# A fused linear-attention and gated-MLP block: GpSimd subtracts the means itself, 29 small operations on other engines, new orders and banks

## The chip, the core and the metric

The kernel runs on one core of a Trainium2 chip. The core has a matrix engine (TensorE, PE in the profile), three elementwise engines (VectorE or DVE, ScalarE or ACT, GpSimd or POOL) and a queue that issues transfers (SyncE, SP). Each engine works through its own list of instructions in order; engines wait for each other on semaphores. The metric is the device time of one execution in microseconds (us).

## The reference, cut to what matters

```
x = A_x                                  # 2048 x 448, bf16
n = layernorm(x)                         # no gain, no bias
q, k, v = split(n @ wqkv)                # 16 heads of 28
phi(t) = where(t > 0, t + 1, exp(t)) + 1e-6
kv  = sum over tokens of phi(k)^T v      # per head
z   = sum over tokens of phi(k)
o   = (phi(q) @ kv) / (phi(q) . z + 1e-6)
h   = x + o @ wo
h2  = h + (gelu(layernorm(h) @ w_gate) * (layernorm(h) @ w_up)) @ w_down
```

`w_gate` and `w_up` are 448 x 1792, `w_down` is 1792 x 448.

## The kernel before, in words

**Tiles.** The 2048 tokens are 16 tiles of 128. 448 columns are three blocks of 128 and one of 64; most products therefore use half of TensorE's rows (64) and run two at a time, one on each half, with a first pass ("a", 8 products) and a second pass ("b", 6 products) that adds to the same two PSUM banks with the halves exchanged. PSUM has eight banks of 128 x 512 f32.

**Tasks and names.** The kernel first builds a graph of 955 tasks. A task has an engine, the buffers that it reads and writes, and a name; on the three elementwise engines a task is one instruction. The names used below, with tile number t:

- `ast`/`aag` t: mean and variance of x (VectorE, L412, L413). `anm`: the negated means of a group (GpSimd, L417), of the tile pairs from tile 2 on. `aln`/`ars`: 1/sqrt(var) by logarithm and exponential (ScalarE, L422, L424).
- `norm` t: (x - mean) * rstd. Tiles 0 and 1 on VectorE (L454, subtract the mean), the others on GpSimd (L457, add the negated mean). `dup` t: for odd tiles, the last 64 columns are copied a second time (L461, L464), as the transposing transfer and the v products need it.
- `tr` t, `ev` t: tiles 0 to 3 are transposed on TensorE (L472 to L474) and copied out of PSUM (VectorE L479 for 0 and 1, ScalarE L481 for 2 and 3). The others go two at a time by a transposing transfer, `xT` (L483).
- `ks` 0, 1 (L506) and `ka`/`kb` t (L519): the k products. `ek` t: exp (ScalarE, L492); `cl` t: clamp to at most 1 (GpSimd, L493); `ph` t: phi(k) (VectorE, L494).
- `g0a`, `g0b`, `g2a`, `g2b` t: the sums over tokens of phi(k) with the normalised x, in four banks (L543). `evg` c copies them out (L568, L570); `zbm`, `evz` spread z over the partitions (L572, L573); `kvp` multiplies by the v weights (L582); `kz1` masks heads (L590); `mm` k multiplies by wo (L601) and `evm` k copies out (L605, L607). So kv and wo become one 448 x 448 matrix.
- `qa`/`qb` t (L620), `eq` t, `cq` t, `pq` t: the same phi for q (L628 to L630).
- `mul` t: phi(q) times z (GpSimd, L660); `den` t, `rd` t: sum per head and reciprocal (VectorE, L662, L663); `om` t: phi(q) divided by the sum (GpSimd, L666).
- `tro`, `evo`, `wo` 0 and 1: transposition on TensorE and product for tiles 0 and 1 (L679 to L694); `oT` (L698), `woa`/`wob` for the other pairs (L705).
- `hr` t: h = x + product (VectorE, L714). `bst`, `bag`: its mean and variance. 1/sqrt for tiles 0 and 1 on ScalarE (`bln`, `brs`), for the pairs after them on GpSimd (`bve`, L429, and `bpw`, a power, L431), with the negated means in `bnm` (L417).
- `normh` t: tiles 0 and 1 on VectorE (L727), then `trh` on TensorE (L734, L736) and `evh` (L739); the others on GpSimd (L746), then `wrap` t, a copy of the last 64 columns (VectorE, L748), and a transposing transfer, `hT` (L749).
- `gua`/`gub` v (L818, L821): gate and up products; `ge` v (ScalarE, L844): gelu; `hm` v (VectorE, L846): times up. The tokens go in chunks of 2, 2, 4, 4 and 4 tiles; v counts 0 to 6 in the first chunk, 7 to 13 in the second, then 14 a chunk.
- `da`/`db` t (L768), `down` (L782), `out` t (VectorE, L788), `dout` t (L790): the down product of a pair of tiles, the last addition and the store. Tiles 14 and 15 go singly, tile 15 in two halves of 224 columns.

**What sets the order.** A list of task numbers for each engine (`ORDERS`, one string each for TensorE, ScalarE, VectorE, GpSimd and SyncE) and a list of banks (`BANKS`, one for each of 196 PSUM tiles), both written into the file. `place` (L155) gives the tasks their order and adds a wait wherever a tile takes a bank that another held: the new product waits for that tile's last reader. `emit` (L204) waits on semaphores by these dependencies and nothing else. Durations and keys in the calls are for the planner that made the lists and change nothing at run time.

**Around the start.** TensorE first does nine products of ones (`warm`, L407), then the four transpositions in the order tr2, tr0, tr1, tr3, then ks1, ks0, ka2, kb2, qa0, qb0, qa2, qb2, ka4, g0a0, kb4. VectorE's list begins with the memset of a part of xn (`xones`, L382, L383), and has that of kvT (`kvzero`, L385, 128 x 1248) behind ph13.

**Around the end of attention.** TensorE: ... kvp qa8 mm0 mm3 mm1 tro1 mm2 qb8 wo1 tro0 qa10 wo0 qb10 qa14 qa12 qb14 qb12 trh1 trh0 woa2 gua3. VectorE: ... den1 rd1 kz1 pq7 den0 pq4 rd0 evm1 den3 pq5 rd3 hr1 bst1 den2 bag1 rd2 pq8 hr0 bst0 pq9 bag0 pq10 normh1 normh0 pq11 evh1. GpSimd: ... cq6 mul1 cq7 mul0 cq4 om1 mul3 cq5 om0 mul2 cq8 om3 om2 cq9 cq10 cq11 mul6 mul7 cq13 cq14 cq12 cq15 om6 mul5 om7 mul4 bve2 bnm2 bpw2 normh2 normh3.

Of the kernel before, what the change touches and what calls it, by code (L numbers as in the profile page):

```python
# [235 lines left out]
def bass_sequential_preLN__linear_attn_block__glu_gated_geglu__prompt_kernel(  # L236
# [27 lines left out]
    with es:
# [657 lines left out]
```

## Time and profile before

| | us |
|---|---|
| median of 3 runs | 194.56 (194.43 to 195.72) |
| the profiled execution | 192.99 |
| its span on the core, from the first instruction to the last | 191.3 |
| TensorE busy | 185.3 |
| VectorE busy | 120.0 |
| GpSimd busy | 78.8 |
| ScalarE busy | 66.5 |

Times in the profile count from the start of the span. L12 is line 12 of the kernel file. A row of the timeline has the start, the duration, the engine, the line, the operation, what it writes and reads, and in brackets the idle time of the engine before it and what ended it; neighbouring instructions of one kind stand in one row (x3). A row of the groups has the busy time of all, the mean of one in ns, and the idle time of the engine before them. In the table by stretch each engine has its busy time and, in brackets, its number of instructions. Ends of products are modelled: two products that follow each other overlap in the rows, so the distance from one start to the next is what a product takes.

### The profile page before, as it was taken

What the parts mean: (1) busy time and instruction counts of PE and PEld (TensorE: products, weight loads), DVE (VectorE), ACT (ScalarE), POOL (GpSimd) and SP (SyncE); (2) the same over time, 40 slices, a digit from 0 to 9 for tenths busy, and PEclk for the clock granted to TensorE, in tenths of its full rate; (3) what the DMA queues carried; (4) which work ended last, traced back from release to release, by engine and by line L of the source; (5) the groups of instructions that cost most, each with busy time, mean ns of one, the idle gap of its engine ahead of it and who ended that gap; (6) DMA issues with size and microseconds to landing.
All of it is one profiled execution on the core that took longest, in us unless ns stands there. A gap on an engine that the chain in (4) does not pass through costs nothing.

```text
span 191.3 us, 4853 instructions
## 1 busy us (share of the span) xinstructions
PE 185.3 (97%) x1939; PEld 108.9 (57%) x1939; DVE 120.0 (63%) x303; ACT 66.5 (35%) x188; POOL 78.8 (41%) x133
## 2 busy tenths in 40 slices
PE   7899999999899999999999999999999999999994
PEld 2334545444499897865555556555555555555643
DVE  4979737598998998387956634374745144345332
ACT  3675624465645241200234330041542321232200
POOL 2899864399899927870129400004600000000000
PEclk9999999999999999999999999999999999999999
DMA  5999589903785122523000382000650000002033
GB/s 139 251 231 176 108 146 319 299 10 87 194 220 122 32 51 48 55 57 55 0 3 0 75 132 28 0 3 0 30 107 26 5 0 0 3 0 72 3 132 108
DMA packets 32694, 15.93 MB, mean 83 GB/s; under 512 B 21536, under 2 KB 32416, under 8 KB 32672
## 3 DMA queue, kind: packets, MB, share of 16 engines
q1 hardware_dynamic: 32672, 15.63, 36.9%
q8 instruction: 15, 0.25, 0.5%
q14 instruction: 7, 0.06, 0.1%
HBM read 8.37 MB, written 1.84 MB: 53 GB/s over the span
## 4 chain that ended last, share of the span: by engine, by line
PE 91%; DVE 4%; POOL 1%; DMA 1%; issue 1%; ACT 0%; POOLq 0%; DVEq 0%
PE ps L818 39%; PE ps L768 19%; PE ps L543 6%; PE ps L821 5%; PE ps L519 5%; PE ps L705 5%; PE ps L620 4%; PE ps L782 3%; DVE st L412 1%; DMA x_sb<-in_A_x_dram 1%; PE ps L506 1%; PE ps L601 1%; POOL xn L457 1%; DVE pq L630 1%; DVE hn L727 1%
## 5 line engine op out<-in xcount | busy, mean ns | idle before, releaser
L821 PE MATMUL ps<-hnT,wgu_sb 64*128 64x512 bf16 (+1 forms) x490 | 87.1, 333 | 0.0
L818 PE MATMUL ps<-hnT,wgu_sb 64*128 64x512 bf16 (+1 forms) x490 | 87.1, 333 | 0.0
L844 ACT ACTIVATE gl<-ps 128x256 bf16<-128x256 f32 x112 | 35.9, 384 | 88.7 <-PE ps L821 56.9
L846 DVE TENSOR_TENSOR hh<-ps,gl 128x256 bf16<-128x256 f32 x112 | 42.1, 415 | 36.2 <-ACT gl L844 35.7
L818 PEld LDWEIGHTS ps<-hnT,wgu_sb 64*128 64x128 bf16 x490 | 46.0, 94 | 30.7 <-issue 0.4
L821 PEld LDWEIGHTS ps<-hnT,wgu_sb 64*128 64x128 bf16 x490 | 45.9, 94 | 0.1
L768 PE MATMUL ps<-wd_sb,hh 64*128 64x448 bf16 x392 | 39.4, 349 | 0.0
L768 PEld LDWEIGHTS ps<-wd_sb,hh 64*128 64x128 bf16 x392 | 22.0, 94 | 15.0 <-issue 0.2
L412 DVE BATCH_NORM_STATS2 st<-x_sb 128x6 f32<-128x448 bf16 x32 | 19.0, 615 | 2.1 <-DMA x_sb<-in_A_x_dram 1.9
L666 POOL TENSOR_TENSOR o<-pq,rd 128x448 bf16<-128x448 bf16 x16 | 15.0, 944 | 12.3 <-DVE rd L663 11.8
L417 POOL TENSOR_SCALAR nm<-mv 128x2 f32<-128x2 f32 (+1 forms) x15 | 3.5, 232 | 32.9 <-DVE mv L413 32.6
L660 POOL TENSOR_TENSOR prod<-pq,zb 128x448 f32<-128x448 bf16 x16 | 16.4, 1034 | 0.0
L788 DVE TENSOR_TENSOR x_sb<-ps,x_sb 128x448 bf16<-128x448 f32 (+1 forms) x17 | 9.9, 590 | 10.1 <-PE ps L768 5.1
L543 PE MATMUL ps<-pk,xn 64*128 64x448 bf16 (+1 forms) x128 | 15.2, 351 | 0.4 <-DVE pk L494 0.4
L494 DVE SCALAR_TENSOR_TENSOR pk<-ps,tm 128x448 bf16<-128x448 f32 x16 | 9.6, 617 | 6.3 <-POOL tm L493 2.5
L714 DVE TENSOR_TENSOR x_sb<-ps,x_sb 128x448 bf16<-128x448 f32 x16 | 9.6, 608 | 6.1 <-PE ps L705 5.6
L620 PE MATMUL ps<-wq_sb,xnT 64*128 64x448 bf16 x112 | 12.7, 350 | 0.1
L519 PE MATMUL ps<-wk_sb,xnT 64*128 64x448 bf16 x98 | 11.8, 350 | 0.1
L705 PE MATMUL ps<-m_sb,oT 64*128 64x448 bf16 x98 | 11.1, 349 | 0.0
L492 ACT ACTIVATE e<-ps 128x448 bf16<-128x448 f32 x16 | 8.0, 540 | 8.3 <-PE ps L519 7.6
L493 POOL TENSOR_SCALAR tm<-e 128x448 bf16<-128x448 bf16 x16 | 8.8, 561 | 4.5 <-ACT e L492 4.4
L457 POOL TENSOR_SCALAR xn<-x_sb,nm,rs 128x448 bf16<-128x448 bf16 x14 | 10.0, 720 | 1.4 <-ACT rs L424 0.9
(80 smaller groups left out, 148.8 us busy)
## 6 DMA issues: line engine op xcount, KB each, us to landing
out_dram<-x_sb SPq DMA_DIRECT2D x15, 112.0 KB, 1.8
wd_sb<-in_B_w_down_dram SPq DMA_DIRECT2D x3, 448.0 KB, 5.1
wgu_sb<-in_B_w_gate_dram SPq DMA_DIRECT2D x3, 384.0 KB, 7.8
wgu_sb<-in_B_w_up_dram SPq DMA_DIRECT2D x3, 384.0 KB, 4.1
x_sb<-in_A_x_dram SPq DMA_DIRECT2D x2, 448.0 KB, 4.6
x_sb<-in_A_x_dram SPq DMA_DIRECT2D x4, 112.0 KB, 2.1
x_sb<-in_A_x_dram SPq DMA_DIRECT2D x2, 224.0 KB, 3.5
wo_sb<-in_A_wo_dram SPq DMA_DIRECT2D x1, 392.0 KB, 7.5
```

The costliest lines, as they stand in the source:

```text
L412: op("dve", lambda e: e.bn_stats(st[:, t, :], src_ap()), [b_src], [b_st[t]], nm + "st%d" % t, 0.615, key)
L519: ins = e.matmul(ps[:, p_k[n].bank, 0:D], xnT[rows, t0 + n, k, :], wk_sb[rows, k, :], start=(k == 0 and not second), stop=(second and k == ...
L543: ins = e.matmul(ps[0:b - a, p_gx[cc].bank, 0:D], xnv(t, a, b)[rows], pk[rows, i, :], start=(t == 0 and not second), stop=(t == T - 1), sk ...
L620: ins = e.matmul(ps[:, p_q[n].bank, 0:D], xnT[rows, ts[n], k, :], wq_sb[rows, k, :], start=(k == 0 and not second), stop=(second and k == ...
L660: op(me, lambda e, ip=ip, p3=p3: e.tensor_tensor(prod[:, ip, :, 0:28], p3(), zb[:].rearrange("p (a e) -> p a e", e=28), ALU.mult), [b_pq[t ...
L666: return e.tensor_tensor(o2[:, so, n, :].rearrange("p (a e) -> p a e", e=28), p3(), rd[:, i, :].unsqueeze(2).to_broadcast([128, 16, 28]), ...
L705: ins = e.matmul(ps[:, p_h[n].bank, 0:D], oT2[rows, so, kk, :], m_sb[rows, kk, :], start=(k == 0 and not second), stop=(second and k == 2) ...
L768: ins = e.matmul(ps[:, p_d[n].bank, 0:D], hh[rows, j, u * 128:(u + 1) * 128], wd_sb[rows, j, :], start=(j == 0 and not second), stop=(j == ...
L818: e.matmul(ps[:, pa.bank, jj * N:(jj + 1) * N], wgu_sb[A_, wa + k if k < 3 else 3, jc], hnT[A_, k, c0:c0 + N], start=(k == 0 and jj == 0 a ...
L821: ins = e.matmul(ps[:, pb.bank, jj * N:(jj + 1) * N], wgu_sb[B_, wb + k if k < 3 else 3, jc], hnT[B_, k, c0:c0 + N], start=(k == 0 and jj ...
L844: G.add("act", lambda e, gi=gi, cs=cs, p_g=p_g: e.activation(gl[:, gi, cs], ps[:, p_g.bank, cs], AF.Gelu_apprx_tanh), r=[p_g], w=[b_gl[gi] ...
L846: op("dve", lambda e, dst=dst, gi=gi, cs=cs, p_u=p_u, rs_=rs_: e.tensor_tensor(dst, rs_(ps[:, p_u.bank, cs]), rs_(gl[:, gi, cs]), ALU.mult ...
```

## The change

Four things change, and nothing else in what is computed.

1. GpSimd's normalisations subtract the mean and multiply, with the mean itself as operand. The negated means (`anm`, `bnm`, 15 instructions on GpSimd) and their buffers go; 940 tasks are left.
2. 29 tasks get another engine, by name (`ENGINE`). From VectorE to GpSimd: norm0, norm1, dup1, normh1. From GpSimd to VectorE: norm2, norm15, cl3, cl8, cl13, cl14, cq4, cq5, cq6, normh2, normh4, normh7. From VectorE to ScalarE: ev0, evg0, evm1, wrap2 to wrap7. From ScalarE to VectorE: ev2, ev3, evz. From ScalarE to GpSimd: dup15.
3. All five orders are new. The start of VectorE's list is now: the memset for prod, kvzero, ast2 ast0 aag2 aag0 ast1 aag1 ast3 aag3 norm2 ast4 ast5 xones aag5 aag4 ev1 ev2 ev3. GpSimd begins with norm0 norm1 norm3 norm5 norm4 cl0 cl1 norm7 dup1 cl2 norm6; its `powwarm` (a first use of the power, L387) moves from before norm3 to before bve2. TensorE: warm tr0 tr2 tr1 ks0 tr3 ks1 ka2 kb2 qa0 g0a0 qb0 qa2 g0b0 qb2 ka4 g0a1 kb4; later ka10 g0b7 g2b7 kb10 g2a8 (before: ka10 g0b7 g2b7 g0a8 g2a8 kb10); then qb6 g0b13 g0a14 zbm g0b14 g0a15 g0b15 qa4 kvp qb4 qa8 mm1 mm2 mm0 tro1 mm3 qb8 tro0 wo1 qa10 wo0 qb10 qa14 qa12 qb14 qb12 trh1 trh0 woa2 gua3. VectorE there: ... evg2 evz cq6 pq7 pq6 den1 kz1 rd1 den0 cq4 rd0 den3 cq5 rd3 pq5 pq4 den2 rd2 hr1 pq9 bst1 hr0 bag1 bst0 pq8 bag0 den6 pq11 normh0 pq10 evh1, and later bag2 bag3 hm3_1 hm3_0 hm0_0 hm0_1 normh2 hm2_1 hm2_0. GpSimd there: cq7 mul1 mul0 mul3 om1 om0 mul2 om3 cq9 om2 cq8 mul6 cq11 cq10 normh1 mul7 cq12 cq14 cq15 om6 cq13 om7 powwarm bve2 bpw2 normh3 mul4 mul5 mul8. SyncE fetches tile 1 of x before tile 3, and issues the transfers of the later weights in another order, some of them later.
4. The banks are new.

The diff, cut to its core (orders and banks left out):

```diff
+ENGINE = (
+    "norm0:pool ev0:act norm1:pool dup1:pool norm2:dve ev2:dve ev3:dve cl3:dve norm15:dve dup15:pool cl8:dve cl13:dve"
+    " cl14:dve evg0:act evz:dve evm1:act cq4:dve cq5:dve cq6:dve normh1:pool normh2:dve wrap2:act wrap3:act normh4:dve"
+    " wrap4:act wrap5:act wrap6:act normh7:dve wrap7:act"
+)
...
+    ENGINE_OF = dict(p.split(":") for p in cfg.get("engine", ENGINE).split())
+
+    def at(name, default):
+        return ENGINE_OF.get(name, default)
+
+    def copy_on(e, eng, o, x):
+        return e.activation(o, x, AF.Identity) if eng == "act" else e.tensor_copy(o, x)
...
-        def ln_negm(ts, mv, nm, b_mv, b_nm, name, key):
-            a, b = ts[0], ts[-1] + 1
-            op("pool", lambda e: e.tensor_scalar(nm[:, a:b], mv[:, a:b, 0], -1.0, None, ALU.mult),
-               b_mv[a:b], b_nm[a:b], name + "%d" % a, 0.225, key)
...
-                if t < N_DVE_NORM:
-                    op("dve", lambda e, t=t: e.tensor_scalar(xnv(t, 0, D), x_sb[:, t, :], mv1[:, t, 0:1], rs1[:, t:t + 1], ALU.subtract, ALU.mult),
-                       [b_x[t], b_mv1[t], b_rs1[t]], [b_xn[sx]], "norm%d" % t, 0.38, kln + 0.05)
-                else:
-                    op("pool", lambda e, t=t: e.tensor_scalar(xnv(t, 0, D), x_sb[:, t, :], nm1[:, t:t + 1], rs1[:, t:t + 1], ALU.add, ALU.mult),
-                       [b_x[t], b_nm1[t], b_rs1[t]], [b_xn[sx]], "norm%d" % t, 0.715, kln + 0.05)
+                ne = at("norm%d" % t, "dve" if t < N_DVE_NORM else "pool")
+                op(ne, lambda e, t=t: e.tensor_scalar(xnv(t, 0, D), x_sb[:, t, :], mv1[:, t, 0:1], rs1[:, t:t + 1], ALU.subtract, ALU.mult),
+                   [b_x[t], b_mv1[t], b_rs1[t]], [b_xn[sx]], "norm%d" % t, 0.40 if ne == "dve" else 0.715, kln + 0.05)
...
-            op("pool", lambda e: e.tensor_scalar(tm1[:, ie, :], e1[:, ie, :], 1.0 + EPS, 0.0, ALU.min, ALU.max), [b_e1[ie]], [b_tm1[ie]], "cl%d" % t, 0.56, kk + 0.3)
+            op(at("cl%d" % t, "pool"), lambda e: e.tensor_scalar(tm1[:, ie, :], e1[:, ie, :], 1.0 + EPS, 0.0, ALU.min, ALU.max), [b_e1[ie]], [b_tm1[ie]], "cl%d" % t, 0.56 if at("cl%d" % t, "pool") == "pool" else 0.45, kk + 0.3)
...
-                ln_negm(list(ts), mv2, nm2, b_mv2, b_nm2, "bnm", k2 + 0.32)
...
+                ne = at("normh%d" % t, "dve" if first else "pool")
+                op(ne, lambda e, t=t, sh=sh: e.tensor_scalar(hn[:, sh, 0:D], h_sb[:, t, :], mv2[:, t, 0:1], rs2[:, t:t + 1], ALU.subtract, ALU.mult),
+                   [b_h[t], b_mv2[t], b_rs2[t]], [b_hn[sh], b_hnd[sh]], "normh%d" % t, 0.59 if ne == "dve" else 0.715, k3)
...
-                    op("dve", lambda e, sh=sh: e.tensor_copy(hn[:, sh, D:512], hn[:, sh, 384:D]), [b_hn[sh]], [b_hnd[sh]], "wrap%d" % t, 0.25, k3 + 0.01)
+                    we = at("wrap%d" % t, "dve")
+                    op(we, lambda e, sh=sh, we=we: copy_on(e, we, hn[:, sh, D:512], hn[:, sh, 384:D]), [b_hn[sh]], [b_hnd[sh]], "wrap%d" % t, {"dve": 0.35, "act": 0.255, "pool": 0.26}[we], k3 + 0.01)
```

The other copies out of PSUM (`ev`, `evg`, `evz`, `evm`, `evo`, `evh`), the clamps `cq`, `dup`, `mul` and `om` look their engine up in the same way.

More of the change, by code (lines that the diff above doesn't have):

```diff
@@ L477, in ln_group @@
                     src = lambda p_t=p_t: psb[:, p_t.bank, 0:512].rearrange("p (k t) -> p k t", k=4)
-                    if t in EV_DVE:
-                        op("dve", lambda e, t=t, src=src: e.tensor_copy(xnT[:, t, :, :], src()), [p_t], [b_xnT[t]], "ev%d" % t, 0.41, kln + 0.12)
-                    else:
-                        op("act", lambda e, t=t, src=src: e.activation(xnT[:, t, :, :], src(), AF.Identity), [p_t], [b_xnT[t]], "ev%d" % t, 0.6, kln + 0.12)
+                    ee = at("ev%d" % t, "dve" if t in EV_DVE else "act")
+                    op(ee, lambda e, t=t, ee=ee, src=src: copy_on(e, ee, xnT[:, t, :, :], src()), [p_t], [b_xnT[t]], "ev%d" % t, 0.41 if ee == "dve" else 0.6, kln + 0.12)
                 elif t % 2:
@@ L566, in bass_sequential_preLN__linear_attn_block__glu_gated_geglu__prompt_kernel @@
             r_ = 128 if c < 3 else 65
-            if c in EVG_DVE:
-                op("dve", lambda e, c=c, r_=r_: e.tensor_copy(gx[0:r_, c, :], ps[0:r_, p_gx[c].bank, 0:D]), [p_gx[c]], [b_gx[c]], "evg%d" % c, 0.62, 27.0 + 0.1 * EVG.index(c))
-            else:
-                op("act", lambda e, c=c, r_=r_: e.activation(gx[0:r_, c, :], ps[0:r_, p_gx[c].bank, 0:D], AF.Identity), [p_gx[c]], [b_gx[c]], "evg%d" % c, 0.546, 27.0 + 0.1 * EVG.index(c))
+            ge = at("evg%d" % c, "dve" if c in EVG_DVE else "act")
+            op(ge, lambda e, c=c, r_=r_, ge=ge: copy_on(e, ge, gx[0:r_, c, :], ps[0:r_, p_gx[c].bank, 0:D]), [p_gx[c]], [b_gx[c]], "evg%d" % c, 0.62 if ge == "dve" else 0.546, 27.0 + 0.1 * EVG.index(c))
         p_zb = G.psum("zb")
         G.add("pe", lambda e: e.matmul(ps[:, p_zb.bank, 0:D], ones_bf[64:65, :], gx[64:65, 3, :], start=True, stop=True), r=[b_ones, b_gx[3]], w=[p_zb], name="zbm", dur=_pe(D, 1, 64), key=27.3, mode=64)
-        op("act", lambda e: e.activation(zb[:], ps[:, p_zb.bank, 0:D], AF.Identity), [p_zb], [b_zb], "evz", 0.546, 27.4)
+        ze = at("evz", "act")
+        op(ze, lambda e: copy_on(e, ze, zb[:], ps[:, p_zb.bank, 0:D]), [p_zb], [b_zb], "evz", 0.62 if ze == "dve" else 0.546, 27.4)
         p_kv = G.psum("kv")
@@ L658, in a2_pair @@
                 p3 = lambda t=t: pq[:, t, :].rearrange("p (a e) -> p a e", e=28)
-                me, se = ("dve" if t in MUL_DVE else "pool"), ("dve" if t in SCL_DVE else "pool")
+                me, se = at("mul%d" % t, "pool"), at("om%d" % t, "pool")
                 op(me, lambda e, ip=ip, p3=p3: e.tensor_tensor(prod[:, ip, :, 0:28], p3(), zb[:].rearrange("p (a e) -> p a e", e=28), ALU.mult), [b_pq[t], b_zb], [b_prod[ip]], "mul%d" % t,
-                   0.60 if me == "dve" else 1.035, k0)
+                   1.30 if me == "dve" else 1.035, k0)
                 op("dve", lambda e, i=i, ip=ip: e.tensor_reduce(den[:, i, :], prod[:, ip, :, :], mybir.AxisListType.X, ALU.add), [b_prod[ip], b_prc], [b_den[i]], "den%d" % t, 0.62, k0 + 0.1)
@@ L738, in a2_pair @@
                     G.add("pe", ftrh, r=[b_hn[sh], b_ident], w=[p_th], name="trh%d" % t, dur=0.40, key=k3 + 0.1)
-                    cp = (lambda e, o, x: e.activation(o, x, AF.Identity)) if t % 2 == 0 else (lambda e, o, x: e.tensor_copy(o, x))
-                    tk = op("act" if t % 2 == 0 else "dve",
-                            lambda e, t=t, p_th=p_th, cp=cp: cp(e, hnT[:, :, (t % HR) * 128:(t % HR + 1) * 128], psb[:, p_th.bank, 0:512].rearrange("p (k t) -> p k t", k=4)),
-                            [p_th], [b_hnT[t % HR]], "evh%d" % t, 0.59 if t % 2 == 0 else 0.41, k3 + 0.2)
-                    if t % 2 == 0:
+                    he = at("evh%d" % t, "act" if t % 2 == 0 else "dve")
+                    tk = op(he, lambda e, t=t, p_th=p_th, he=he: copy_on(e, he, hnT[:, :, (t % HR) * 128:(t % HR + 1) * 128], psb[:, p_th.bank, 0:512].rearrange("p (k t) -> p k t", k=4)),
+                            [p_th], [b_hnT[t % HR]], "evh%d" % t, 0.59 if he == "act" else 0.41, k3 + 0.2)
+                    if he == "act":
                         exp_tasks.append(tk)
                 else:
-                    op("pool", lambda e, t=t, sh=sh: e.tensor_scalar(hn[:, sh, 0:D], h_sb[:, t, :], nm2[:, t:t + 1], rs2[:, t:t + 1], ALU.add, ALU.mult),
-                       [b_h[t], b_nm2[t], b_rs2[t]], [b_hn[sh], b_hnd[sh]], "normh%d" % t, 0.715, k3)
-                    op("dve", lambda e, sh=sh: e.tensor_copy(hn[:, sh, D:512], hn[:, sh, 384:D]), [b_hn[sh]], [b_hnd[sh]], "wrap%d" % t, 0.25, k3 + 0.01)
+                    we = at("wrap%d" % t, "dve")
+                    op(we, lambda e, sh=sh, we=we: copy_on(e, we, hn[:, sh, D:512], hn[:, sh, 384:D]), [b_hn[sh]], [b_hnd[sh]], "wrap%d" % t, {"dve": 0.35, "act": 0.255, "pool": 0.26}[we], k3 + 0.01)
                     G.add("sp", lambda e, t=t, sh=sh: e.dma_start_transpose(hnT[:, :, (t % HR) * 128:(t % HR + 1) * 128], hn[:, sh, :]), r=[b_hn[sh], b_hnd[sh]],
```

39 lines of the change are left out of this document (12 added, 27 removed), and 77 rows, old and new, of tables (BANKS, ORDERS).

## The prediction, made before the result was known

> **What bounds the kernel now.** I read the page first, then the busy time of each engine by stretch, then TensorE's timeline, then the chain of waits.
>
> ```profile
> span 191.3 us, 4853 instructions
> PE 185.3 (97%) x1939; PEld 108.9 (57%) x1939; DVE 120.0 (63%) x303; ACT 66.5 (35%) x188; POOL 78.8 (41%) x133
> ```
>
> ```profile
> core 0: us, PE busy (x) PEld busy (x) DVE busy (x) ACT busy (x) POOL busy (x), PEclk, DMA share, GB/s
> 0.00:5.60 5.60, 4.02 (x9) 1.20 (x9) 3.00 (x11) 2.28 (x5) 1.80 (x12) 1.00 0.59 161
> 5.60:9.50 3.90, 3.57 (x27) 1.63 (x27) 3.89 (x14) 2.73 (x10) 3.15 (x7) 1.00 0.91 247
> 9.50:20.00 10.50, 10.30 (x102) 4.71 (x103) 9.29 (x24) 7.07 (x22) 10.27 (x20) 1.00 0.99 198
> 20.00:32.00 12.00, 11.61 (x124) 6.07 (x120) 6.50 (x14) 4.94 (x14) 7.72 (x16) 1.00 0.77 172
> 40.00:52.50 12.50, 11.54 (x97) 5.21 (x92) 11.91 (x26) 7.75 (x18) 11.72 (x16) 1.00 0.42 105
> 52.50:185.00 132.50, 132.50 (x1480) 83.47 (x1479) 78.19 (x209) 37.35 (x114) 39.82 (x59) 1.00 0.23 44
> 185.00:191.30 6.30, 3.79 (x27) 2.42 (x25) 1.91 (x4) 0.00 (x0) 0.00 (x0) 1.00 0.36 121
> ```
>
> TensorE is the bound. From 52.5 to 185 us it has no idle time at all and its clock is granted in full, so engines and orders can't shorten that part; they can only break it. The last stretch is the final products, the last addition and its store: the change leaves the last three products and the last store in their places. What can move lies before 52.5 us, where attention ends and the gate/up products (L818, L821) start, and where VectorE (11.91 of 12.50 us) and GpSimd (11.72) are full as well. So I ask one thing: when does the first gate/up product (52.52 us) start after the change?
>
> ```profile
> 5.62 0.34 PE L472 MATMUL ps<-ident,xn 128*128 128x128 bf16 x3 [0.53 <-POOL xn L457]
> 6.07 0.34 PE L472 MATMUL ps<-ident,xn 128*128 128x128 bf16 x3
> 7.88 2.00 PE L506 MATMUL ps<-wk_sb,xnT 128*128 128x448 bf16 x8
> 9.53 1.92 PE L519 MATMUL ps<-wk_sb,xnT 64*128 64x448 bf16 x14
> 11.29 3.29 PE L620 MATMUL ps<-wq_sb,xnT 64*128 64x448 bf16 x28
> 14.41 0.92 PE L519 MATMUL ps<-wk_sb,xnT 64*128 64x448 bf16 x8
> 18.73 0.93 PE L519 MATMUL ps<-wk_sb,xnT 64*128 64x448 bf16 x8
> 19.49 0.55 PE L543 MATMUL ps<-pk,xn 64*128 64x448 bf16 x4
> 25.97 0.55 PE L543 MATMUL ps<-pk,xn 64*128 64x448 bf16 x4 [0.39 <-DVE pk L494]
> 50.09 0.34 PE L734 MATMUL ps<-ident,hn 128*128 128x128 bf16 x3 [0.44 <-DVE hn L727]
> 51.11 0.34 PE L734 MATMUL ps<-ident,hn 128*128 128x128 bf16 x3 [0.51 <-DVE hn L727]
> 52.52 0.27 PE L818 MATMUL ps<-hnT,wgu_sb 64*128 64x256 bf16 x1
> ```
>
> Starts tell more than durations, which overlap. Eight 64-row products take 19.49 - 18.73 = 0.76 us when nothing holds them, 0.095 us each. The 28 q products from 11.29 to 14.41 take 3.12 us where 28 x 0.095 = 2.66 would do. And the rows with brackets are waits for VectorE's phi (L494) and for the normalised h (L727).
>
> **The change, part by part.** Prices, by form:
>
> ```profile
> L417 POOL TENSOR_SCALAR nm<-mv 128x2 f32<-128x2 f32 x13 | 2.9, 225 | 30.1 <-DVE mv L413 29.8
> L457 POOL TENSOR_SCALAR xn<-x_sb,nm,rs 128x448 bf16<-128x448 bf16 x14 | 10.0, 720 | 1.4 <-ACT rs L424 0.9 <-PE ps L543 0.3 <-POOL nm L417 0.2
> L454 DVE TENSOR_SCALAR xn<-x_sb,mv,rs 128x448 bf16<-128x448 bf16 x2 | 0.7, 374 | 0.0
> L727 DVE TENSOR_SCALAR hn<-x_sb,mv,rs 128x448 bf16<-128x448 bf16 x2 | 2.0, 1052 | 0.0
> L493 POOL TENSOR_SCALAR tm<-e 128x448 bf16<-128x448 bf16 x16 | 8.8, 561 | 4.5 <-ACT e L492 4.4
> L479 DVE COPY xnT<-ps 128x512 bf16<-128x512 bf16 x2 | 0.7, 403 | 0.0
> L568 DVE CAST gx<-ps 128x448 bf16<-128x448 f32 x2 | 1.2, 625 | 1.1 <-PE ps L543 1.1
> L748 DVE COPY hn<-hn 128x64 bf16<-128x64 bf16 x14 | 5.5, 397 | 4.6 <-POOL hn L746 4.4
> ```
>
> *Negated means.* Fifteen instructions of about 0.225 us go, 3.4 us of GpSimd. GpSimd's subtract-and-multiply is shown nowhere; the nearest row is its add-and-multiply, 0.72 us, the clamp with two constants at 0.56 us is the other bound, and I take 0.72. Since this time lies beside a full TensorE, it is worth something only where GpSimd ends last: the row of L457 shows 0.2 us of waiting for nm in all. Term: 0, at most -0.2.
>
> *The same VectorE instruction has two prices.* L454 and L727 have the same operation and shape, yet take 0.374 and 1.052 us. The timeline says why:
>
> ```profile
> 48.87 2.05 POOL L660 TENSOR_TENSOR prod<-pq,zb 128x448 f32<-128x448 bf16 x2
> 49.03 2.03 DVE L727 TENSOR_SCALAR hn<-x_sb,mv,rs 128x448 bf16<-128x448 bf16 x2
> 60.72 2.02 POOL L660 TENSOR_TENSOR prod<-pq,zb 128x448 f32<-128x448 bf16 x2
> 60.79 1.00 DVE L748 COPY hn<-hn 128x64 bf16<-128x64 bf16 x1
> 134.22 2.15 POOL L746 TENSOR_SCALAR hn<-x_sb,nm,rs 128x448 bf16<-128x448 bf16 x3
> 135.68 0.18 DVE L748 COPY hn<-hn 128x64 bf16<-128x64 bf16 x1
> ```
>
> Behind a GpSimd TENSOR_TENSOR (mul, om) a VectorE copy or scale between SBUF tensors ends only about when that ends; beside a GpSimd TENSOR_SCALAR it takes its 0.18 us. So a clamp (cl, cq) or norm moved to VectorE costs 0.37 us where GpSimd runs one-input work and up to 1.05 us behind a mul or om; a clamp on VectorE stands in no row, and these are its bounds. The Trainium skill ("SBUF — State Buffer", section "Who interferes with whom") says that such a VectorE instruction and any GpSimd instruction share one pair of ports as an exclusive lock, held for the whole instruction by whoever starts first; the rows agree for two inputs and not for one (0.18 us at 135.68), and what the page would make of the time is among the rivals.
>
> *Start, to the first paired k product (9.53).* norm0 and norm1 go to GpSimd, norm2 to VectorE, and tr0 leads. Statistics of tile 0 end about 0.12 us behind those of tile 2, and GpSimd's norm takes 0.72, so the first transposes start near 5.80, not 5.62. They follow each other at 6.07 - 5.62 = 0.45 us, and ks0 needs only ev0 (ScalarE): tr0, tr2, tr1, then ks0 at 7.15 instead of ks1 at 7.88. The eight solo products last 9.53 - 7.88 = 1.65 us, with tr3 now between them 2.1. First pair near 9.3: **-0.2** (bounds +0.2, the later start alone, and -0.4).
>
> *Second passes (11.29 to 14.41).* qb0 directly behind qa0 adds to the same two banks; that is where the surplus of 3.12 - 2.66 = 0.46 us is. The new order puts g0a0 and g0b0 between, whose inputs (ph0, ph1) I find ready near 11.0 and 11.6: **-0.4** (0 to -0.46).
>
> *14.4 to 25 us.* VectorE gets ev2, ev3 (0.40 each) and cl3 (0.37 or more), 1.2 us; it loses norm0, norm1 (0.374 each) and dup1, 0.9 us. The kvT memset and prod's go to its idle time before the first statistics. In that stretch VectorE is busy 9.29 of 10.50 us, so phi 4 to 7 come no earlier though TensorE arrives 0.6 us sooner: TensorE waits before ka6 and for ph6, ph7: **+0.3** (0 to +0.6).
>
> *25 to 32 us.* kb10 (six products, 0.57 us) goes ahead of g2a8, which waited for ph8 (25.97; by starts 0.55 us lost); cl8, cl13, cl14 and norm15 move to VectorE, where 6.50 of 12.00 us are busy and GpSimd runs no TENSOR_TENSOR yet: **-0.5** (-0.2 to -0.6).
>
> *32 to 40 us.* g0b13 to g0b15 come before qa4, so the sums end earlier; qb4 fills the wait for kvT. But evg0 joins evg1 on ScalarE, and VectorE does evz (0.62) and cq6 ahead of kz1: **-0.3** (0 to -0.6).
>
> *40 to 52.5 us.* The end here is VectorE's chain.
>
> ```profile
> 44.20 0.64 DVE x_sb L714
> 49.23 0.73 issue
> 49.96 1.11 DVE hn L727
> ```
>
> From hr1 (44.20) to the end of normh0 (51.07) it is 6.87 us. normh1 goes to GpSimd (0.72 there, beside VectorE's work; it is queued behind mul6, cq11, cq10, ahead of mul7) and takes 1.0 us out; den2 and rd2 move ahead of hr1; den6 and pq11 come in. That is some 1.2 us shorter. Against it, cq4 and cq5 stand on VectorE between den0 and pq5, exactly while GpSimd runs om1, om0, mul2: each ends when that operation ends, behind them rd0, rd3, pq5 and pq4 are queued, and wo1's bank is freed only by pq5. At one wait apiece wo1 and hr1 come 0.6 us sooner than now instead of 1.15 us, and the first gate/up product would start 1.5 us sooner than now. Every further miss of the gap between two GpSimd operations costs up to 1.0 us (L727's row against L454's: 0.7); over four such instructions (cq4, cq5, cq6, normh0) I count 0.4. Term: **0.0** (-0.4 to +1.0).
>
> *After 52.5 us.* wrap2 to wrap7 (0.18 to 1.7 us each on VectorE) go to ScalarE, which is 37.35 of 132.50 us busy; normh2, normh4, normh7 come the other way. No term, as long as TensorE stays fed: what hides these edits is the queue of gate/up products, and if normh2 is late the cover is gone (second rival).
>
> Sum: -0.2 - 0.4 + 0.3 - 0.5 - 0.3 + 0.0 = **-1.1 us**. The profiled execution (span 191.3, execution 192.99) becomes 190.2 and 191.9. The median of the runs, 194.56, is 1.6 above that execution; the same 1.1 us off gives **193.4 us**.
>
> **Rivals.** First, *the gain is larger*: VectorE's fast instructions fit the gaps and the phi waits of 14 to 25 us don't come. Terms at their good ends: -0.4 - 0.46 + 0 - 0.6 - 0.6 - 0.4 = -2.5, so 192.1 us. For it: each is a wait that the trace shows. Against: they all need VectorE in time, and it is full.
>
> Second, *slower*: normh2 now stands on VectorE ahead of hm2_1 and hm2_0, which free the two banks of gua5, and mul4, mul5, mul8 follow normh3 on GpSimd. If normh2 starts after mul4 does, it waits 1.0 us, or 2.0 if it misses the gap; wrap2 and wrap3 on ScalarE, ge6 and ge1 behind them, and hT2/hT3 wait too, and the full stretch gets its first hole. It decides when the four products ahead of normh2 (0.34 us apart) and its wait for rstd take longer than normh3's 0.72 us. With the middle at its bad end (+1.0) and the hole at 2.0: -1.1 + 1.0 + 2.0 = +1.9, near 196.5 us. Against: by my walk normh2 starts 0.5 us before mul4.
>
> Third, *nothing moves*: the early lead is eaten at phi 4 to 7 and by cq4 and cq5, and hr1 comes when it does now: within 0.3 of 194.6 us. For it: VectorE and GpSimd at 11.9 and 11.7 of 12.5 us.
>
> Fourth, *one-input work blocks too*: norm2 waits behind norm0 and norm1 to 6.5 us, cl3, cl8, cl13, cl14 behind GpSimd's norms and clamps by 0.3 us or so each; the start loses 0.2 and the waits for phi add up to 0.8: 193.4 + 1.0 = 194.4 us. The copy at 135.68 speaks against it. This is what the lock on the Trainium skill's page "SBUF — State Buffer" would do.
>
> **How the numbers follow.** Forecast (gain 0.4 to 1.9): 0.50. Larger gain: 0.23. Nothing or the lock for one-input work: 0.18. Slower: 0.09. One per cent is 1.95 us, about what a measurement of this kernel can tell from no change: faster by more 0.24 (the first rival and an edge of the forecast), slower by more 0.08, within it 0.68. The range leaves out the last tenth on either side: 191.8 to 195.3; the forecast's own is 192.6 to 194.2.
>
> **What would show it.** Right: first paired k product near 9.3, ka4 near 14.2 with g0a0 and g0b0 done, no gap ahead of g2a8, wo1 near 42.6, first gate/up product between 51.0 and 51.8, and TensorE full from there to 185. Also cq4 and cq5 at 0.5 to 1.1 us but cl3, cl8, cl13, cl14 near 0.4. Wrong: idle time of TensorE after 52.5 us waiting for hh or hnT (second rival); cl8 or norm2 at 0.7 us and more (fourth); a first gate/up product at 52 or later (third) or before 50.7 us (first).

## The result, and the profile after

The changed kernel takes 210.7 us (median of 4 runs, 210.25 to 212.64), where the kernel before takes 194.73 (4 runs of the same session). The ratio is 1.083, with a 95% interval of 1.075 to 1.091. The forecast was 193.4. The profiled execution took 211.01 us, with a span of 209.3 where the kernel before had 191.3: 18.0 us more. Executions of one and the same kernel can lie about 3 us apart, which a median mixes, so the ratios and the profiled executions are compared below.

The head of the page after, and TensorE's granted clock in 40 slices:

```profile
span 209.3 us, 4843 instructions
PE 190.2 (91%) x1939; PEld 119.0 (57%) x1939; DVE 120.3 (57%) x305; ACT 67.0 (32%) x193; POOL 100.6 (48%) x111
PEclk9759998799999999999999999999999999999999
```

GpSimd has 22 instructions fewer than before and is busy 21.8 us longer (100.6 against 78.8). The table of groups says why; these are GpSimd's norms of the first and of the second LayerNorm (the columns after the bar are busy us, mean ns of one, idle us before them):

```profile
L453 POOL TENSOR_SCALAR xn<-x_sb,mv,rs 128x448 bf16<-128x448 bf16 x14 | 25.9, 1859 | 3.8 <-ACT rs L425 3.8
L712 POOL TENSOR_SCALAR hn<-x_sb,mv,rs 128x448 bf16<-128x448 bf16 x12 | 22.5, 1877 | 0.6 <-ACT gl L828 0.2
```

A norm that took 0.72 us takes 1.86. Over 26 of them that is 26 x 1.14 = 29.6 us of GpSimd, against 3.4 us saved by the negated means. Busy time by stretch (columns as in the prediction's table) shows where it lands:

```profile
5.60:9.50 3.90, 1.52 (x15) 0.92 (x15) 1.99 (x9) 1.55 (x6) 3.90 (x4) 0.82 0.86 232
9.50:20.00 10.50, 10.43 (x73) 3.76 (x75) 6.42 (x16) 4.91 (x14) 10.42 (x10) 0.74 0.44 111
20.00:32.00 12.00, 7.88 (x78) 3.30 (x76) 6.98 (x16) 3.71 (x12) 12.00 (x14) 1.00 0.30 57
120.00:140.00 20.00, 16.71 (x168) 9.77 (x166) 10.37 (x26) 2.63 (x8) 4.57 (x3) 1.00 0.22 44
140.00:160.00 20.00, 18.21 (x175) 9.16 (x171) 9.12 (x28) 6.47 (x20) 9.26 (x8) 1.00 0.16 34
```

From 5.6 to 32 us GpSimd (the fifth busy time) is busy 26.32 of 26.40 us: in the first LayerNorm it has become the bound, and TensorE waits for it. The second loss stands in 120 to 160 us, where TensorE had no idle time before: 3.29 and 1.79 us are missing. In the timeline the first paired k product starts at 13.27 us instead of 9.53, and the first gate/up product at 64.53 instead of 52.52. So 12.0 of the 18.0 us are lost ahead of the first gate/up product, and 6.0 behind it, 5.1 of these in the two stretches above:

```profile
13.27 2.71 PE L510 MATMUL ps<-wk_sb,xnT 64*128 64x448 bf16 x14
64.53 0.27 PE L802 MATMUL ps<-hnT,wgu_sb 64*128 64x256 bf16 x1
```

The later holes are read engine by engine. Here are, of the same timeline, GpSimd's norms, VectorE's next copy or multiplication, and TensorE's next product, for both holes:

```profile
118.08 5.58 POOL L712 TENSOR_SCALAR hn<-x_sb,mv,rs 128x448 bf16<-128x448 bf16 x3
123.70 1.00 DVE L268 COPY hn<-hn 128x64 bf16<-128x64 bf16 x2 [1.68 <-POOL hn L712]
124.61 1.74 DVE L830 TENSOR_TENSOR hh<-ps,gl 128x256 bf16<-128x256 f32 x5
126.07 0.93 PE L691 MATMUL ps<-m_sb,oT 64*128 64x448 bf16 x8 [2.87 <-DVE hh L830]
...
148.15 5.55 POOL L712 TENSOR_SCALAR hn<-x_sb,mv,rs 128x448 bf16<-128x448 bf16 x3
153.74 0.35 DVE L268 COPY hn<-hn 128x64 bf16<-128x64 bf16 x3 [3.56 <-POOL hn L712]
154.80 0.39 PE L805 MATMUL ps<-hnT,wgu_sb 64*128 64x512 bf16 x1 [1.79 <-DVE hh L830]
```

GpSimd is not full here (4.57 and 9.26 of 20 us). What is late is a short run of three norms, 5.6 us instead of 2.2. VectorE works in order: the copy of the last columns (`wrap`) waits for the norm, the multiplications (`hm`, L830) that empty the PSUM banks stand behind it, and TensorE waits for a bank.

### The profile page after: what moved, and what is told of

Its sections match the earlier page's. It is cut to its first block, busy times and chain, and to the rows that moved or that the text cites. A ratio compares the mean times of both kernels' runs of the same rounds, so it can differ in the third digit from the quotient of the medians.

```text
span 209.3 us, 4843 instructions
## 1 busy us (share of the span) xinstructions
PE 190.2 (91%) x1939; PEld 119.0 (57%) x1939; DVE 120.3 (57%) x305; ACT 67.0 (32%) x193; POOL 100.6 (48%) x111
## 5 line engine op out<-in xcount | busy, mean ns | idle before, releaser
L830 DVE TENSOR_TENSOR hh<-ps,gl 128x256 bf16<-128x256 f32 x112 | 41.6, 414 | 36.8 <-ACT gl L828 36.6
L752 PE MATMUL ps<-wd_sb,hh 64*128 64x448 bf16 x392 | 40.6, 349 | 0.0
L752 PEld LDWEIGHTS ps<-wd_sb,hh 64*128 64x128 bf16 x392 | 26.0, 94 | 11.2 <-issue 0.2
L453 POOL TENSOR_SCALAR xn<-x_sb,mv,rs 128x448 bf16<-128x448 bf16 x14 | 25.9, 1859 | 3.8 <-ACT rs L425 3.8
L712 POOL TENSOR_SCALAR hn<-x_sb,mv,rs 128x448 bf16<-128x448 bf16 x12 | 22.5, 1877 | 0.6 <-ACT gl L828 0.2
L534 PE MATMUL ps<-pk,xn 64*128 64x448 bf16 (+1 forms) x128 | 16.4, 362 | 4.1 <-DVE pk L485 3.0
L418 DVE BATCH_NORM_STATS2 st<-x_sb 128x6 f32<-128x448 bf16 x32 | 18.9, 613 | 0.7 <-DMA x_sb<-in_A_x_dram 0.5
L430 POOL TENSOR_SCALAR ln<-mv 128x2 f32<-128x2 f32 x7 | 1.6, 228 | 34.7 <-DVE mv L419 34.7
L510 PE MATMUL ps<-wk_sb,xnT 64*128 64x448 bf16 x98 | 13.8, 396 | 2.1 <-DVE pk L485 2.0
L534 PEld LDWEIGHTS ps<-pk,xn 64*128 64x128 bf16 (+1 forms) x128 | 6.4, 101 | 12.3 <-DVE pk L485 3.4
```

Of the source, the lines that this page charges most:

```text
L418: op("dve", lambda e: e.bn_stats(st[:, t, :], src_ap()), [b_src], [b_st[t]], nm + "st%d" % t, 0.615, key)
L453: op(ne, lambda e, t=t: e.tensor_scalar(xnv(t, 0, D), x_sb[:, t, :], mv1[:, t, 0:1], rs1[:, t:t + 1], ALU.subtract, ALU.mult), [b_x[t], b_ ...
L510: ins = e.matmul(ps[:, p_k[n].bank, 0:D], xnT[rows, t0 + n, k, :], wk_sb[rows, k, :], start=(k == 0 and not second), stop=(second and k == ...
L534: ins = e.matmul(ps[0:b - a, p_gx[cc].bank, 0:D], xnv(t, a, b)[rows], pk[rows, i, :], start=(t == 0 and not second), stop=(t == T - 1), sk ...
L712: op(ne, lambda e, t=t, sh=sh: e.tensor_scalar(hn[:, sh, 0:D], h_sb[:, t, :], mv2[:, t, 0:1], rs2[:, t:t + 1], ALU.subtract, ALU.mult), [b ...
L752: ins = e.matmul(ps[:, p_d[n].bank, 0:D], hh[rows, j, u * 128:(u + 1) * 128], wd_sb[rows, j, :], start=(j == 0 and not second), stop=(j == ...
```

## The experiments

Theory 1: GpSimd's TENSOR_SCALAR takes 1.86 us as soon as it subtracts, and the whole loss follows from that. Theory 2: it is dear because its operand is now the mean, read from a column of the statistics. Theory 3: the new engines, orders and banks are at fault.

**One word changed in the changed kernel** (e1_add_mean):

```
-    ... rs1[:, t:t + 1], ALU.subtract, ALU.mult)
+    ... rs1[:, t:t + 1], ALU.add if ne == "pool" else ALU.subtract, ALU.mult)
(the same in the second LayerNorm)
```

> The changed kernel with one word different: GpSimd's 26 norms add the mean instead of subtracting it (so those tiles are normalised to (x + mean) * rstd, not the reference's value). Engines, orders, banks, operands and the absence of negated means stay. Theory 1 (the subtract form itself is dear on GpSimd, 1.86 us against 0.72, and all the loss follows from it): the two GpSimd norm rows show 0.72 us, the first gate/up product comes near 51.4 us, TensorE has no hole after it, total 193.4 (191.8 to 195.5). Theory 2 (dear because the mean is read from a strided column of the statistics): the rows stay at 1.86 us and the total at 210.7. Theory 3 (new engines, orders and banks are at fault): the rows show 0.72 us and the total is 200 or more.

Profiled execution 191.76 us (span 190.0); median 194.62 of 10 runs, ratio 0.9947 (0.9867 to 1.0028): all of the loss is gone, and against the kernel before no difference can be told. The norms of each LayerNorm on GpSimd, with minimum, median and maximum of one in ns:

```profile
L453 POOL TENSOR_SCALAR xn<-x_sb,mv,rs x14: 711/718/1872, 5.1 to 23.2; 128x448 bf16<-128x448 bf16 x14
...
L712 POOL TENSOR_SCALAR hn<-x_sb,mv,rs x12: 717/718/1875, 47.8 to 131.3; 128x448 bf16<-128x448 bf16 x12
```

The edit reads the engine's name late, so one norm in each LayerNorm still subtracted, and three of VectorE's added. Those two took 1872 and 1875 ns among neighbours at 718, with the same operands and orders. Theory 3 falls, and theory 2 too, since the mean's column is still the operand.

**The first part of the change alone** (e2_sub_alone), in the kernel before:

```
-   op("pool", ... nm1[:, t:t + 1], rs1[:, t:t + 1], ALU.add, ALU.mult)
+   op("pool", ... mv1[:, t, 0:1], rs1[:, t:t + 1], ALU.subtract, ALU.mult)
(the same in the second LayerNorm; the 15 tasks anm and bnm are gone)
```

> The kernel before with the first part of the change alone: no negated means, GpSimd subtracts the mean itself; engines, orders and banks of before. It has 27 GpSimd norms (12 of them in the second LayerNorm) and 15 fewer small operations. Theory 1: the norm rows show 1.86 us, and the total is 200 to 213. Theory 2: the same rows and the same total as theory 1. Theory 3: the total is 194 to 195.5, as before.

215.9 us, ratio 1.1105 (1.1026 to 1.1185), more than theory 1 said, and 28 norms instead of the 27 named there:

```profile
L455 POOL TENSOR_SCALAR xn<-x_sb,mv,rs 128x448 bf16<-128x448 bf16 x14 | 26.0, 1862 | 3.5 <-DVE mv L413 3.5
L743 POOL TENSOR_SCALAR hn<-x_sb,mv,rs 128x448 bf16<-128x448 bf16 x14 | 26.1, 1869 | 0.3
```

The first part of the change alone loses some 21 us. With the new engines, orders and banks the loss is smaller: the spans are 214.1 and 209.3 us.

**The disputed price by itself** (probe_forms): one GpSimd instruction after the other, nothing else at work.

```
+ e.tensor_scalar(o, x, mean, one, ALU.subtract, ALU.mult)   # and 13 more forms, 3 of each
```

> No part of the reference is computed (the output is x): GpSimd runs fourteen forms of one operation on 128 partitions of bfloat16, three times each, with no other engine at work, then VectorE runs two of them. Theory 1: every form with a subtract in it takes 1.86 us at 448 elements, whether the mean comes from the strided column, from a column of its own or is a constant, and whether the subtract stands first, second or alone; every form without one takes 0.56 to 0.72; at 224 elements the subtract takes about half of 1.86; VectorE takes about 0.37 for both. Theory 2: 1.86 only where the operand is the mean's column (the add of it too), 0.72 with the other column.

```profile
L230 POOL TENSOR_SCALAR p_mulsub<-x_sb,rs,mv 128x448 bf16<-128x448 bf16 x3 | 5.6, 1865 | 0.3
L226 POOL TENSOR_SCALAR p_submul<-x_sb,mv,rs 128x448 bf16<-128x448 bf16 x3 | 5.6, 1862 | 0.3
L227 POOL TENSOR_SCALAR p_submul_neg<-x_sb,nm,rs 128x448 bf16<-128x448 bf16 x3 | 5.6, 1862 | 0.3
L233 POOL TENSOR_SCALAR p_subconst<-x_sb 128x448 bf16<-128x448 bf16 x3 | 5.1, 1713 | 0.3
L232 POOL TENSOR_SCALAR p_add<-x_sb,nm 128x448 bf16<-128x448 bf16 x3 | 4.2, 1406 | 0.3
L231 POOL TENSOR_SCALAR p_sub<-x_sb,mv 128x448 bf16<-128x448 bf16 x3 | 4.2, 1404 | 0.3
L237 POOL TENSOR_TENSOR p_ttsub<-x_sb 128x448 bf16<-128x448 bf16 x3 | 3.1, 1030 | 0.2
L238 POOL TENSOR_TENSOR p_ttadd<-x_sb 128x448 bf16<-128x448 bf16 x3 | 3.1, 1028 | 0.2
L229 POOL TENSOR_SCALAR p_muladd<-x_sb,rs,nm 128x448 bf16<-128x448 bf16 x3 | 2.2, 718 | 0.3
L228 POOL TENSOR_SCALAR p_addmul_mean<-x_sb,mv,rs 128x448 bf16<-128x448 bf16 x3 | 2.2, 718 | 0.3
L225 POOL TENSOR_SCALAR p_addmul<-x_sb,nm,rs 128x448 bf16<-128x448 bf16 x3 | 2.2, 717 | 9.2 <-DVE rs L213 9.0
L234 POOL TENSOR_SCALAR p_clamp<-x_sb 128x448 bf16<-128x448 bf16 x3 | 1.7, 561 | 0.2
L239 DVE TENSOR_SCALAR v_submul<-x_sb,mv,rs 128x448 bf16<-128x448 bf16 x3 | 1.2, 397 | 53.7 <-POOL p_ttadd L238 53.7
L240 DVE TENSOR_SCALAR v_addmul<-x_sb,nm,rs 128x448 bf16<-128x448 bf16 x3 | 1.2, 397 | 0.1
```

Theory 2 is out: add with the mean's column 718 ns, subtract with the other column 1862. Theory 1 holds for pairs of operations: subtract first or second, or with constants, 1.71 to 1.87 us. As a law about every form it was too wide, twice: an add alone, 1406 ns, costs as much as a subtract alone, twice the pair of add and multiply; and with two tensors there is no difference (1030, 1028). So what is cheap are certain pairs, add and multiply, multiply and add (718), minimum and maximum (561); why these, no run shows. VectorE takes 397 ns either way. From 224 columns (1112 and 531 ns, two further rows of this view) to 448 the subtract grows by 0.75 us and the add by 0.19.

**Negated means back, in the new orders** (e3_negm_dve), made by VectorE:

```
+   op("dve", lambda e: e.tensor_scalar(nm[:, a:b], mv[:, a:b, 0], -1.0, None, ALU.mult), ...)
    (17 tasks behind bn_aggr; GpSimd's norms: nm, ALU.add, ALU.mult)
```

> The changed kernel's engines, orders and banks, with negated means back, made by VectorE right behind the statistics (17 small operations), and GpSimd's norms adding them: the reference's values. Theory 1: GpSimd norm rows at 0.72 us, the 17 small operations under 0.1 us each, first gate/up product near 51.5 us, total 193.6 (192 to 195.5), within 0.5 of the kernel in which GpSimd adds the mean. Theory 2: also 0.72 us and about 193.6, since the operand is no longer the strided column. Theory 3: 200 or more.

Median 194.2, ratio 0.999 (0.9937 to 1.0043). The rows are at 726 and 730 ns. But the profiled execution took 195.54 where 193.6 was expected: ka2 starts at 11.62 us and not near 9.3. From ka4 to the first gate/up product (54.72) this trace lies 3.5 to 3.8 us behind that of e1_add_mean: what is lost is lost at the start. Two things lie there, and this run does not tell them apart. The 17 small operations take about 0.2 us each, not under 0.1, and one of them stands ahead of norm2 in VectorE's list. And TensorE's first products are slow (granted clock 0.73 between 5.6 and 9.5 us); e5_add_all below has slow first products too, and its first gate/up product at 54.26, without any of the small operations.

**The same with the early ones on GpSimd** (e4_negm_mix):

```
-   op("dve", ...
+   op("pool" if name == "anm" and a < 6 else "dve", ...
```

> The changed kernel's engines, orders and banks, with negated means back: those of the first six row tiles on GpSimd, which stands idle there while ScalarE works out the reciprocal deviation, the other 13 on VectorE right behind the statistics; GpSimd's norms add them. The reference's values. Theory 1, with the delay of the start in the run before told apart: GpSimd norm rows at 0.72 us; second k product ka2 at 9.3 to 9.5 us and TensorE's clock granted in full there (in the run with all negated means on VectorE ka2 began at 11.62 us and the granted clock was 0.73 between 5.6 and 9.5 us); first gate/up product at 51.2 to 52.0; a profiled execution of 191.9 to 192.7 us against 193.0 of the kernel before; ratio of the timed runs 0.99 to 1.0. If instead VectorE's small operations in the middle cost the 3.6 us, ka2 comes at 9.4 but the first gate/up product near 54 and the time near 195.

Profiled execution 192.35, median 192.46 (192.11 to 195.48), ratio 0.9907 (0.9852 to 0.9961): about 1% below the kernel before, with the reference's values. ka2 starts at 9.51, the first gate/up product at 51.41, 0.20 and 0.32 us behind e1_add_mean. So VectorE's small operations in the middle cost about 0.1 us.

**Every norm adding** (e5_add_all): `ne=ne` bound in both lambdas of e1_add_mean.

> The changed kernel with every one of GpSimd's 26 norms adding the mean instead of subtracting it (those tiles become (x + mean) * rstd). In the first such run 24 of the 26 did, since the edit read the engine's name late, and the two that went on subtracting (the profile's 23.17 and 72.32 us) took 1.87 us each. Theory 1: all 26 rows at 0.72 to 0.83, total 191.0 to 192.0 in the profiled execution, ratio 0.99 to 0.995. Theory 3: 195 or more.

Rows at 719 and 724 ns, ratio 0.9884 (0.9804 to 0.9963). The expectation of 191 to 192 in the profiled execution missed: it took 195.13, with slow first products (the last section shows them); the lowest run took 191.8.

**The loss split by LayerNorm** (e6_sub_first, e7_sub_second): e5_add_all with the subtract left in one of the two.

> GpSimd subtracts in the first LayerNorm (14 norms, as the change has it) and adds the mean in the second (12 norms, not the reference's values there). Theory 1: the rows show 1.86 and 0.72; the first gate/up product comes near 63 to 64.5 us, where the changed kernel has it (64.53), and TensorE has no hole after it: 203 to 205.5. If the later holes follow from the late start instead of the second LayerNorm's price: near 210.

> GpSimd adds the mean in the first LayerNorm (not the reference's values there) and subtracts in the second (12 norms, as the change has it). Theory 1: the rows show 0.72 and 1.86; the first gate/up product comes at 51.1 to 53 us, and TensorE has holes of 3.1, 2.0 and 0.6 us after it, as the changed kernel has: 197 to 199.5. The two parts, 12 us and 6 us, then add up to the 18 us lost. If the holes follow from the late start instead: 192 to 193.

The first gate/up product of e7_sub_second, and its hole:

```profile
54.77 0.27 PE L802 MATMUL ps<-hnT,wgu_sb 64*128 64x256 bf16 x1
116.27 1.68 PE L691 MATMUL ps<-m_sb,oT 64*128 64x448 bf16 x8 [2.87 <-DVE hh L830]
```

With the subtract in the first LayerNorm: 204.25 us, ratio 1.052 (1.0435 to 1.0605), span 202.4, 12.4 more than e1_add_mean's 190.0, all of it by the first gate/up product (63.45 against 51.09), and TensorE has no hole after it. With the subtract in the second there were two runs only. The profiled one, 202.19 us, has e5_add_all's slow first products, so its first gate/up product (54.77) and its time miss the expectation; the other, 198.21 us with a span of 196.5, fits it, and is 6.5 more than e1_add_mean's 190.0. The same 2.87 us hole as in the changed kernel stands in the profiled run though its chain starts 10 us earlier: it belongs to the price, not to the late start. 12.4 + 6.5 = 18.9, against 209.3 - 190.0 = 19.3 for both together.

**Is it the clock?** The changed kernel's clock row is low at the start (0.82 and 0.74). In e10_after_warm16 more of the warm-up products of ones keep TensorE busy up to its first transposes:

```
-    WARM = cfg.get("warm", 9)
+    WARM = cfg.get("warm", 16)
```

> The changed kernel, subtracting, with 16 warm-up products instead of 9, which fill TensorE's idle time up to the first transposes at 7.1 us. It tells apart whether the 12 us lost ahead of the first gate/up product are GpSimd's queue itself or TensorE's low granted clock at the start (0.82 and 0.74 between 5.6 and 20 us). Theory 1 (GpSimd's queue, busy 22.4 of 22.5 us between 9.5 and 32): ka2 comes up to 1.5 us earlier than 13.27, but g2a8 stays near 38.4, the first gate/up product near 64.5, total 209.5 to 211. Rival (the clock): the first gate/up product at 60 or earlier, total 206 or less.

```profile
9.50:20.00 10.50, 8.26 (x71) 3.24 (x71) 6.33 (x16) 4.58 (x13) 10.42 (x9) 1.00 0.43 110
```

212.25 us (two runs), ratio 1.0912 (1.0752 to 1.1072), span 209.8; both runs are above the 209.5 to 211 of theory 1, and far above the rival's 206. The clock is 1.00 there, TensorE does its work in 8.26 us instead of 10.43, GpSimd is as full as ever (10.42 of 10.50), and the first gate/up product comes at 64.2 us instead of 64.5. So the low clock is not what the 12 us were lost to.

**More warm-up where it can help**: 11 products in e4_negm_mix (e8_negm_mix_warm11) and in the kernel before (e9_before_warm11).

> The kernel with negated means back (six tiles on GpSimd, the rest on VectorE), with 11 warm-up products on TensorE instead of 9. The two more fill the idle time from 4.9 to 5.8 us, ahead of the first transposes. In two runs so far TensorE's transposes of the start took 0.68 us a group instead of 0.45 and the first k product 1.72 instead of 0.97, up to about 14 us, and the first gate/up product came 3 us later with the same work done; the profile's own clock row was at full there. If that is a clock which rises only after a busy stretch of TensorE, long enough, the filled gap makes the quick start the rule: median 191.8 to 192.6 with few runs near 195, ratio 0.985 to 0.99, against 192.46 and 0.9907 with 9. If the pace of the start is set by something else: the same mix as with 9.

> The kernel before with 11 warm-up products instead of 9, nothing else. The first transposes start 5.62 us here, so the two more end about 0.1 us behind that at most. If TensorE's pace at the start hangs on its being busy: ratio 0.985 to 0.998, the scatter of the runs (192.8 to 197.0 so far) gets smaller. If not: ratio 0.998 to 1.003.

The first: 192.41 us, all six runs between 192.29 and 192.55, ratio 0.9891 (0.9817 to 0.9965): the best version here. The second: 193.16, twelve runs between 192.73 and 194.03, ratio 0.9952 (0.9912 to 0.9993), while the kernel before ran from 192.76 to 196.29 beside them. Both expectations held in their numbers. Their picture of a filled gap did not: in the trace of e8_negm_mix_warm11 TensorE still stands idle for 0.54 us ahead of the first transposes, 0.71 in e4_negm_mix. Between the two medians, 0.75 us are left for the new engines, orders and banks.

**Three clamps back on GpSimd** (e11_cq_back), in e4_negm_mix:

```
-    cq4:dve cq5:dve cq6:dve            (ENGINE)
+    GpSimd: cl15 cq6 cq7 mul1 mul0 mul3 cq4 om1 cq5 om0 mul2
```

> The kernel with negated means back (six tiles on GpSimd, the rest on VectorE), with the clamps cq4, cq5 and cq6 on GpSimd again (cq6 ahead of cq7, cq4 behind mul3, cq5 behind om1) instead of on VectorE, where they took 0.88, 0.74 and 0.27 us in the stretch from 38 to 42 us. By the prediction's term for 40 to 52.5 us (0.0, from -0.4 to +1.0) the move to VectorE is worth next to nothing: the first gate/up product comes within 0.5 us of the 51.41 of the kernel with the clamps on VectorE. If GpSimd is the bound there (busy 11.4 of 12.5 us): 0.6 to 1.5 us later and a total of 193.0 to 194.0 in the profiled execution, against 192.35.

Median 196.72, ratio 1.0107 (1.0032 to 1.0182). The stretch where the end of attention lies, with the clamps back, and the same without:

```profile
40.00:52.50 12.50, 11.39 (x101) 5.13 (x98) 10.62 (x24) 7.74 (x18) 12.50 (x17) 1.00 0.38 85
```

```profile
40.00:52.50 12.50, 11.95 (x113) 5.96 (x111) 12.43 (x29) 8.98 (x22) 11.34 (x16) 1.00 0.61 159
```

GpSimd is then busy for all of the 12.50 us. From the start of kvp to the first gate/up product it is 54.87 - 39.31 = 15.56 us, against 51.41 - 37.66 = 13.75: in these two traces, one of each kernel, the three clamps on VectorE are worth 1.8 us. That is above either expectation. The other 1.65 us of the difference stand ahead of kvp, where the lists differ by cq6 alone and the granted clock was 0.85 and 0.89 between 5.6 and 20 us; why all six runs of this kernel took 195.8 us or more stays open.

## Why the prediction was wrong

**The step that failed** is the term *Negated means*: "GpSimd's subtract-and-multiply is shown nowhere; the nearest row is its add-and-multiply, 0.72 us, the clamp with two constants at 0.56 us is the other bound, and I take 0.72." It was set at "0, at most -0.2" and is worth +19.3 us: 1.86 instead of 0.72 us, 26 times, 12.4 us of it ahead of the first gate/up product. The other half of the step failed with it: the time was to lie "beside a full TensorE", and at that price GpSimd ended last (busy 26.32 of 26.40 us from 5.6 to 32) and TensorE waited. The two bounds lay on one side, both below what came. The page had farther rows to bound it from above: GpSimd's TENSOR_TENSOR took 1.03 us. Even that would have been too low, but 26 x 0.3 = 8 us on an engine busy 10.27 of 10.50 us would have put a slower case with a price into the range. None of the rivals had this mechanism.

**The sum of the other terms held**, as the kernel with the price that I took shows. These are the starts in e1_add_mean of ka2, ka4, g2a8, wo1 and the first gate/up product:

```profile
9.31 1.92 PE L510 MATMUL ps<-wk_sb,xnT 64*128 64x448 bf16 x14
...
14.19 0.54 PE L510 MATMUL ps<-wk_sb,xnT 64*128 64x448 bf16 x4
...
25.51 0.55 PE L534 MATMUL ps<-pk,xn 64*65 64x448 bf16 x4
...
42.71 0.55 PE L680 MATMUL ps<-m_sb,oT 128*128 128x448 bf16 x2
...
51.09 0.27 PE L802 MATMUL ps<-hnT,wgu_sb 64*128 64x256 bf16 x1
```

Forecast were 9.3, 14.2, no gap ahead of g2a8 (no bracket there), 42.6 and 51.0 to 51.8. TensorE then has no hole (133.91 of 133.91 us busy from 51.09 to 185), and the execution took 191.76 us, where 191.9 was forecast (the median of its runs, 194.62, lies above the 193.4, inside the range of 191.8 to 195.3). e4_negm_mix, which pays for its negated means, took 192.35. The terms between ka4 and kvp were not told apart by any run; kvp is the first place to check their sum. Here it is in the kernel before and in e1_add_mean:

```profile
38.43 0.36 PE L582 MATMUL ps<-gx,wvt_sb 64*112 64x112 bf16 x4
...
37.31 0.36 PE L572 MATMUL ps<-gx,wvt_sb 64*112 64x112 bf16 x4
```

That is 1.12 us sooner, and the terms up to there add up to -1.1.

**The term of 40 to 52.5 us** was 0.0 (-0.4 to +1.0). From kvp to the first gate/up product it is 52.52 - 38.43 = 14.09 us before and 51.09 - 37.31 = 13.78 in e1_add_mean, so the term came out at -0.3, inside its bounds. One part of it had the wrong sign. The clamps cost VectorE about what was forecast, 0.5 to 1.1 us for cq4 and cq5 (0.88 and 0.73); this is the group of all three in e4_negm_mix:

```profile
L630 DVE TENSOR_SCALAR tm<-e 128x448 bf16<-128x448 bf16 x3 | 1.9, 627 | 0.0
```

But the term counted their move as a loss, and the room that they leave on GpSimd had no price in it: e11_cq_back shows the stretch 1.8 us longer with them there.

**The fourth rival** (one-input work on GpSimd blocks VectorE too) does not hold as it stood. These are GpSimd's norm0 and norm1 in the changed kernel, VectorE's norm2 inside them, then a later pair of GpSimd's norms and VectorE's norm15:

```profile
5.19 3.70 POOL L453 TENSOR_SCALAR xn<-x_sb,mv,rs 128x448 bf16<-128x448 bf16 x2 [3.80 <-ACT rs L425]
5.75 0.36 DVE L453 TENSOR_SCALAR xn<-x_sb,mv,rs 128x448 bf16<-128x448 bf16 x1
...
33.73 3.71 POOL L453 TENSOR_SCALAR xn<-x_sb,mv,rs 128x448 bf16<-128x448 bf16 x2
35.29 1.13 DVE L453 TENSOR_SCALAR xn<-x_sb,mv,rs 128x448 bf16<-128x448 bf16 x1 [0.68 <-PE ps L534]
```

norm2 took 0.36 us in the midst of a GpSimd instruction of 1.86, and cl3, cl8, cl13 and cl14 took 0.27 or 0.28 us. The lock for the whole instruction that the Trainium skill ("SBUF — State Buffer", section "Who interferes with whom") describes for VectorE's two-port modes does not show there, though no trace tells which mode norm2 ran in. But norm15, which began shortly before the second of the pair, took 1.13 us; in e1_add_mean, inside a GpSimd subtract that began at 23.17 us, it took 0.40. So something held norm15 beside one-input work, and what it was stays open. The second rival (a hole for lack of normh2) was close in kind, a late norm with a bank behind it, but not in place: TensorE is full from 64.53 to 122 us, what was late was a norm of GpSimd, and the bank waited for a multiplication behind `wrap`.

## What to carry to other kernels

The price of an elementwise instruction can hang on its pair of operations, on one engine and not on another: before swapping add for subtract in a loop, time the exact form once by itself, and if that can't be done, bound it from above too and multiply by the count. An instruction that gets slower on an engine with idle time still costs where another engine's in-order list stands behind it. And undo one word of a large change first: here one word held all of the loss, and the rest of the change, with negated means back, gains 0.4 to 0.9%.
